# A spectral filter with gated convolution: the forward DFT by channel chunks, the rest by blocks of 512 positions, and part of the filter products on GpSimd

## The chip, the cores and the metric

The kernel runs on one core of a Trainium2 chip. The time is the device time of one execution in microseconds; three runs of the kernel before gave 344.11, 345.82 and 351.01 us, and their median is the time before. The engines are called PE (TensorE, matmuls; PEld are its weight loads), DVE (VectorE), ACT (ScalarE), POOL (GpSimd) and SP (SyncE, which here only issues DMAs).

## The reference

```python
# x (8, 3200, 256), filt_r and filt_i (1601, 256), float32
X = np.fft.rfft(x, axis=1)
y = np.fft.irfft(X * (filt_r + 1j * filt_i)[None], n=3200, axis=1)
# then, on y: a causal convolution of 5 taps per channel, as a gate
gate_pre[t] = sum(conv_w[k] * y_padded[t + k] for k in range(5))
gate = 1 / (1 + np.exp(-gate_pre))
out = (gate * (y @ w_val)) @ w_out        # (8, 3200, 256)
```

So each of eight batches is transformed over 3200 positions, multiplied by a filter, transformed back, convolved with a short filter whose sigmoid is a gate, multiplied by a value product, and multiplied by an output matrix.

## The kernel before

The DFT of 3200 points is split into 100 x 32: position n = 32a + r, with a from 0 to 99 and r from 0 to 31 (a phase). A batch goes through these stages, and each has a small function:

- `load_x`: eight loads per batch on the GpSimd queue, each of 4 phases (100 partitions x 4 x 256, cast from float32 to bf16). Tile `xt`, ten buffers.
- `s1`: the DFT over a, for 4 phases at once, two matmuls of 512 columns. Its moving operand is read in runs of 4 channels. `so` copies the result out of PSUM into one tile per batch.
- `turn`: four VectorE transposes of 32 x 32 blocks per batch (float32 words that hold two bf16 values), when all of `so` is there.
- `s2`: the DFT over r, for two of 13 frequency groups at a time (the last time one), so seven chunks `UCH` per batch. Four 64 x 64 matmuls stand side by side in the array. `xs` copies a chunk out of PSUM as bf16.
- `zed`: two products per chunk on VectorE, `za` with the real and `zb` with the imaginary part of the filter, from and to SBUF.
- `inva`: the inverse over one index, 16 matmuls per chunk, accumulated over `za` and `zb`. `ue` copies it out of PSUM, `wr` writes it to a scratch tensor `escr` in DRAM.
- `lv` reads `escr` back with another partition index, when all seven chunks are written; `ib` does the second inverse step for 4 phases at a time, and `ye` (ScalarE) copies y out of PSUM. y is held phase by phase as 36 x 100, the first four phases being a halo that `halo` copies on GpSimd.
- `conv`: 20 matmuls with diagonal matrices per chunk of 4 phases; a chunk needs only its own and the previous chunk of y. `gate` (ScalarE, sigmoid), `val` (matmuls of y with `w_val`), `gv` (VectorE, product of gate and value from PSUM), `outp` (8 matmuls of 256 columns), `oe` (copy out of PSUM) and `store` (two DMAs) follow, eight times per batch.

PSUM has four buffers of 128 x 1024 float32 that all stages take in turn. Copies out of PSUM go through the helper `copy` (L408 on ScalarE, L410 on VectorE), so many stages share one of these two lines.

The order of all instructions on all engines is written before the run: the class `Plan` holds a list of tasks with an assumed cost, the tasks that they depend on, the buffers that they take and give, and a rank. It runs through time with these costs and always takes the ready task of the lowest rank whose engine is free. The functions then emit their instructions in that order, and each engine works through its own in order. Where a copy can go to either engine, the plan chooses. Before the loop, `pool_setup` makes constants on GpSimd, loads batch 0 and the filters; `sp_setup` has SP double the filters in SBUF to the other partitions.

## Time and profile before

| what | value |
|---|---|
| median of three runs | 345.82 us (344.11 to 351.01) |
| the profiled execution's span | 344.8 us |
| PE busy | 288.3 us (84%) |
| ACT busy | 267.8 us (78%) |
| DVE busy | 256.4 us (74%) |
| POOL busy | 68.0 us (20%) |
| DMA, all queues | 70.91 MB, 206 GB/s on average |

The profiled execution's span lies 1.0 us below the median of the runs. The page gives busy times; a group of instructions has its line in the program, its engine, what it writes and reads, how many there are, the busy time and the mean time of one, and behind the bar the idle time of the engine just before them with what ended it. Busy times of neighbouring matmuls overlap, since a matmul's end is modelled, so what a stage costs on PE is better read from start to start in the timeline.

### The profile page before, as it was taken

The numbers are of one execution on the slowest core, as the hardware profiler recorded it, in microseconds if no ns is written. First come the engines' busy times: TensorE is split into PE (matmuls) and PEld (weight loads), VectorE is DVE, ScalarE is ACT, GpSimd is POOL, SyncE is SP. The second block draws the span as 40 slices with busy tenths as digits, with TensorE's granted clock in tenths as the row PEclk, the third lists the DMA queues.
The fourth block names the chain that finished last, engine by engine and source line by source line (L and its number), as shares of the span: only waits on it lengthen the run. The fifth ranks groups of instructions, "written<-read, shape, count | busy, mean of one in ns | idle before, by whom it ended". The sixth has DMA issues, their size and how long they took to land.

```text
span 344.8 us, 9785 instructions
## 1 busy us (share of the span) xinstructions
PE 288.3 (84%) x3988; PEld 191.6 (56%) x3988; DVE 256.4 (74%) x340; ACT 267.8 (78%) x309; POOL 68.0 (20%) x142
## 2 busy tenths in 40 slices
PE   2634677639999987999779997999999999999992
PEld 0023031326667755776457764776577677766762
DVE  4985477938698996889849994989798999734541
ACT  3954286928898987898849986998999789887663
POOL 8687455210112112110211011100100000001000
PEclk9999999969999999899989998999999999999997
DMA  6999999995899989898869969795677568778544
GB/s 95 155 168 163 213 192 195 206 238 168 199 232 247 272 233 231 245 229 251 170 200 207 271 176 250 214 245 171 199 208 221 156 204 261 234 214 248 160 144 143
DMA packets 57421, 70.91 MB, mean 206 GB/s; under 512 B 8608, under 2 KB 37152, under 8 KB 57376
## 3 DMA queue, kind: packets, MB, share of 16 engines
q1 hardware_dynamic: 45344, 55.20, 53.4%
q0 software_dynamic: 12032, 15.08, 29.0%
q8 instruction: 31, 0.51, 0.6%
q14 instruction: 14, 0.11, 0.1%
HBM read 43.78 MB, written 39.85 MB: 243 GB/s over the span
## 4 chain that ended last, share of the span: by engine, by line
PE 43%; DMA 24%; DVE 15%; ACT 7%; issue 4%; POOL 4%; SPq 1%; ACTq 0%; POOLq 0%; DVEq 0%
DMA vt<-escr 13%; PE ps L583 12%; PE ps L545 10%; DMA xt<-in_x_dram 6%; PE ps L563 6%; DVE tt L436 5%; DVE gv L573 5%; PE ps L417 5%; PE ps L518 5%; PE ps L477 4%; DMA fi_t<-in_filt_i_dram 3%; PE ps L446 3%; ACT o L408 2%; DVE xs L410 2%; POOL xt L161 2%
## 5 line engine op out<-in xcount | busy, mean ns | idle before, releaser
L573 DVE TENSOR_TENSOR gv<-ps,gt 128x800 bf16<-128x800 f32 x64 | 62.7, 980 | 19.9 <-PE ps L563 13.6
L408 ACT ACTIVATE o<-ps 100x1024 f32<-100x1024 f32 x59 | 61.0, 1035 | 16.9 <-PE ps L583 12.9
L410 DVE CAST xs<-ps 128x1024 bf16<-128x1024 f32 (+1 forms) x44 | 50.4, 1145 | 29.0 <-PE ps L446 29.0
L583 PE MATMUL ps<-wo_t,gv 128*100 128x256 bf16 x512 | 68.7, 278 | 2.7 <-DVE gv L573 1.1
L545 PE MATMUL ps<-yt,dg_t 64*64 64x400 bf16 x1280 | 67.3, 339 | 0.3
L408 ACT ACTIVATE so<-ps 128x1024 bf16<-128x1024 f32 x53 | 54.5, 1029 | 15.9 <-PE ps L417 11.1
L528 ACT ACTIVATE yt<-ps 128x800 bf16<-128x800 f32 x64 | 53.9, 846 | 15.9 <-PE ps L518 15.7
L583 PEld LDWEIGHTS <-gv 128*100 128x100 bf16 x512 | 54.5, 125 | 18.6 <-DVE gv L573 9.0
L161 POOL DMA_DIRECT2D xt<-in_x_dram x64 | 35.4, 556 | 124.5 <-PE ps L417 119.8
L554 ACT ACTIVATE gt<-ps 128x800 bf16<-128x800 f32 x64 | 54.1, 847 | 6.5 <-PE ps L545 5.3
L417 PE MATMUL ps<-xt,cf_t 100*128 100x512 bf16 x128 | 47.5, 462 | 12.2 <-DMA xt<-in_x_dram 11.2
L563 PE MATMUL ps<-yt,wv_t 128*128 128x400 bf16 x256 | 54.4, 335 | 0.5 <-ACT gt L554 0.5
L408 ACT ACTIVATE u<-ps 128x1024 bf16<-128x1024 f32 (+1 forms) x46 | 44.9, 982 | 7.2 <-PE ps L477 6.6
L518 PE MATMUL ps<-ci_t,vt 104*128 104x100 f16 x512 | 34.3, 212 | 16.5 <-DMA vt<-escr 16.4
L518 PEld LDWEIGHTS <-vt 104*128 104x128 bf16 x512 | 29.6, 100 | 30.1 <-DMA vt<-escr 19.8
L545 PEld LDWEIGHTS <-dg_t 64*64 64x64 bf16 x1280 | 34.5, 108 | 17.3 <-issue 4.2
L436 DVE STREAM_TRANSPOSE tt<-so 128x1024 f32<-128x1024 f32 x32 | 40.6, 1272 | 3.2 <-ACT so L408 3.2
L464 DVE TENSOR_TENSOR za<-xs,fr_t 128x1024 bf16<-128x1024 bf16 (+1 forms) x56 | 36.1, 649 | 1.4 <-ACT xs L408 0.2
L464 DVE TENSOR_TENSOR zb<-xs,fi_t 128x1024 bf16<-128x1024 bf16 (+1 forms) x56 | 35.5, 640 | 1.4 <-DMA fi_t<-in_filt_i_dram 1.4
L477 PE MATMUL ps<-zb,b_t 64*64 64x256 bf16 x416 | 29.7, 294 | 4.4 <-DVE zb L464 4.4
L477 PE MATMUL ps<-za,a_t 64*64 64x256 bf16 x416 | 30.3, 298 | 2.4 <-DVE za L464 2.1
L446 PE MATMUL ps<-tt,w_t 64*64 64x256 bf16 x416 | 24.2, 305 | 9.0 <-DVE tt L436 4.4
(93 smaller groups left out, 181.9 us busy)
## 6 DMA issues: line engine op xcount, KB each, us to landing
out_dram<-o SPq DMA_DIRECT2D x64, 384.0 KB
xt<-in_x_dram POOLq DMA_DIRECT2D x64, 200.0 KB, 6.7
escr<-u SPq DMA_DIRECT2D x48, 256.0 KB
vt<-escr SPq DMA_DIRECT2D x64, 192.0 KB
escr<-u SPq DMA_DIRECT2D x8, 128.0 KB
vt<-escr SPq DMA_DIRECT2D x64, 16.0 KB
out_dram<-o SPq DMA_DIRECT2D x64, 16.0 KB
fr_t<-in_filt_r_dram POOLq DMA_DIRECT2D x8, 56.0 KB, 4.7
```

Of the source, the lines that this page charges most:

```text
L408: nc.scalar.activation(dst, src, AF.Copy, **kw)
L410: nc.vector.tensor_copy(dst, src)
L417: nc.tensor.matmul(ps[:, 512 * h:512 * h + 512], lhsT=cf_t[0:L].rearrange("p h c i -> p (h c i)"), rhs=xv[:, DQ // 2 * h:DQ // 2 * h + DQ ...
L436: nc.vector.transpose(dst, src)
L464: (nc.vector if e == "DVE" else nc.gpsimd).tensor_tensor(z[:, :, 0:nm * D], xs_[:, :, 0:nm * D], f[:, :, m0:m0 + nm, :].rearrange("p h m d ...
L477: nc.tensor.matmul(ps[64 * h:64 * h + 64, 512 * t + D * a:512 * t + D * a + D], lhsT=tab[rows, h, m0 + a, :], rhs=zz[w][rows, h, D * a:D * ...
L518: nc.tensor.matmul(ps[:, o:o + L], lhsT=v[0:NV, a, 128 * dh:128 * dh + 128], rhs=ci_t[0:NV, :], start=True, stop=True)
L545: nc.tensor.matmul(ps[64 * dh:64 * dh + 64, 512 * r:512 * r + RC * L], lhsT=dg_t[rows, dh, k, :], rhs=y[rows, dh, RC * j + k:RC * j + k + ...
L554: nc.scalar.activation(g[...], ps[:, :].rearrange("p (h n) -> p h n", h=2)[:, :, 0:RC * L], AF.Sigmoid)
L563: nc.tensor.matmul(ps[:, 512 * eh:512 * eh + RC * L], lhsT=wv_t[:, dh, 128 * eh:128 * eh + 128], rhs=y[:, dh, H + RC * j:H + RC * j + RC, ...
L573: nc.vector.tensor_tensor(gv_[...], ps[:, :].rearrange("p (h n) -> p h n", h=2)[:, :, 0:RC * L], g[...], op=ALU.mult)
L583: nc.tensor.matmul(ps[0:L, D * a:D * a + D], lhsT=gv_[:, eh, L * a:L * a + L], rhs=wo_t[:, eh, :], start=(eh == 0), stop=(eh == 1))
```

## The change

- A load of x carries 8 phases, so there are four per batch, in six buffers. `s1` takes 32 channels and all 32 phases at a time: eight chunks per batch, each with four matmuls of 256 columns, one for each load. A transpose follows each chunk (eight per batch, of 512 words), with steps that put the result into one tile by frequency.
- The filters' real and imaginary parts stand in one tile, and one instruction forms both products of a chunk. In four of the seven chunks VectorE forms them straight from PSUM, so these chunks have no `xs` copy. In the other three (`ZG`), `xs` is still copied and GpSimd forms them; in batch 0 VectorE forms all seven.
- y is held in the order of the positions, in two tiles with four zeros ahead. `ib` works on 5 or 4 phases at a time (seven steps); the copy out of PSUM scatters its phases. The halo is gone; the scale 1/N has moved into tables.
- `conv`, `gate`, `val`, `gv`, `outp` and `store` work on blocks of 512 or 384 consecutive positions, seven per batch, and a block waits for the whole of y. `gv` writes its result so that `outp` has 128 positions at a step on the partitions: 50 matmuls of 256 columns per batch. A store is one DMA of 128 partitions.
- The plan keeps track of which of four PSUM buffers a task takes, has the DMA engines as an engine of its own, and takes ranks from a table.

```diff
+ZG = (1, 3, 5)
+ICH = [(0, 5), (5, 5), (10, 5), (15, 5), (20, 4), (24, 4), (28, 4)]
+BLK = [(0, 4), (4, 4), (8, 4), (12, 4), (16, 3), (19, 3), (22, 3)]
...
+PAR = dict(
+    PERIOD=20.7,
+    OFF=dict(cv=84.19, ia=48.09, ib=42.46, lv=-355.46, lx=-53.1, op=71.53, s1=-260.24, s2=45.97, vl=-551.16,
+             z=-229.99, zp=386.18),
+    STEP=dict(cv=1.785, ia=0.594, ib=5.658, lv=54.689, lx=0.786, op=8.159, s1=19.782, s2=1.912, vl=8.146,
+             z=1.876, zp=68.373),
+)
...
+    NXT, NSO, NXS, NZ, NU, NVB, NGB, NOB = 6, 3, 3, 3, 4, 4, 3, 4
...
+    f_t = cpool.tile([128, 2, 2, NM, D], BF16, name="f_t")
+    y_t = [cpool.tile([128, 2, H + N], BF16, name=f"y{n}") for n in range(2)]
...
+    def s1(b, q):
         ps = psum()
+        w = R // NX
+        for j in range(NX):
+            nc.tensor.matmul(ps[:, w * CQ * j:w * CQ * j + w * CQ],
                              lhsT=cf_t[0:L].rearrange("p h c i -> p (h c i)"),
+                             rhs=st["X", b, j][0:L, :, CQ * q:CQ * q + CQ],
+                             start=True, stop=True)
...
     def turn(b, q):
+        src = st.pop(("SO", b, q))[...].rearrange("p r w -> p (r w)").bitcast(FP32)
+        dst = st["T", b][...].rearrange("p i d -> p (i d)").bitcast(FP32)
+        V.transpose(dst.rearrange("p (i k) -> p k i", i=32)[:, CQ // 2 * q:CQ // 2 * q + CQ // 2],
+                    src.rearrange("p (r k) -> p k r", r=32))
...
+    def zed(b, u, e):
         m0, nm = UCH[u]
+        if e == "POOL":
+            eng, src = nc.gpsimd, st.pop(("XS", b, u))[:, :, 0:nm * D]
+        else:
+            eng, src = V, st.pop(("s2", b, u))[:, :].rearrange("p (h n) -> p h n", h=2)
+            src = src[:, :, 0:nm * D]
+        z = st["Z", b, u] = zpool.tile([128, 2, 2, 2 * D], BF16, name="z")
+        eng.tensor_tensor(z[:, :, :, 0:nm * D],
+                          src.unsqueeze(1).to_broadcast((128, 2, 2, nm * D)),
+                          f_t[:, :, :, m0:m0 + nm, :].rearrange("p w h m d -> p w h (m d)"),
+                          op=ALU.mult)
...
     def ye(b, i, e):
+        r0, nr = ICH[i]
         ps = st.pop(("ib", b, i))
+        copy(e, y_t[b % 2][:, :, H:H + N].rearrange("p h (n r) -> p h n r", r=R)
+             [:, :, :, r0:r0 + nr],
+             ps[:, :].rearrange("p (h n) -> p h n", h=2)[:, :, 0:nr * L]
+             .rearrange("p h (r n) -> p h n r", n=L))
...
     def conv(b, j):
+        m0, nm = BLK[j]
+                                 rhs=y[rows, dh, 128 * m0 + k:128 * m0 + k + 128 * nm],
...
+        V.tensor_tensor(
+            t[:, :, 0:nm, :].rearrange("p h a n -> p h n a"),
+            ps[:, :].rearrange("p (h n) -> p h n", h=2)[:, :, 0:128 * nm]
+            .rearrange("p h (n a) -> p h n a", a=nm),
+            gt[:, :, 0:128 * nm].rearrange("p h (n a) -> p h n a", a=nm), op=ALU.mult)
...
+        for a in range(nm):
             for eh in range(2):
+                nc.tensor.matmul(ps[:, D * a:D * a + D], lhsT=t[:, eh, a, :],
+                                 rhs=wo_t[:, eh, :], start=(eh == 0), stop=(eh == 1))
...
+        dst = out[b, 128 * m0:128 * m0 + 128 * nm, :].rearrange("(p a) d -> p (a d)", a=nm)
+        nc.sync.dma_start(out=dst, in_=o[:, 0:nm * D])
```

More of the change, by code (lines that the diff above doesn't have):

```diff
@@ L608, with act, dve, two @@
+    add = plan.add
+    def act(n):
+        return 0.2 + 0.00083 * n
+    def dve(n):
+        return 0.16 + 0.00105 * n
+    def two(n):
+        return {"ACT": act(n), "DVE": dve(n)}
+    def rank(s, b, k):
+        return s, b, k
     for b in range(B):
-        t0 = NCH * b
-        for j in range(NCH):
+        for j in range(NX):
             if b:
-                add(f"lx{b},{j}", {"POOL": 0.6}, t0 + j - 9, ["pool"], lambda e, b=b, j=j: load_x(b, j),
-                    take=("xt",), land=5.0)
-            dep = [f"lx{b},{j}"] if b else [f"x0{j}", "cfa"]
-            dep = dep + ([f"s1{b},{j - 1}"] if j else [])
-            add(f"s1{b},{j}", {"PE": 0.45}, t0 + j, dep, lambda e, b=b, j=j: s1(b, j),
-                take=("ps",) + (("so",) if j == 0 else ()), give=("xt",), mode=0)
-            add(f"so{b},{j}", two(0.97, 1.15), t0 + j, [f"s1{b},{j}"],
-                lambda e, b=b, j=j: so(b, j, e), give=("ps",))
@@ L677 @@
-    add("pool", {"none": 0.0}, -100, [], None, land=26.0)
-    add("wts", {"POOL": 8.0}, 8.5, ["pool"], lambda e: load_w())
-    for j in range(NCH):
-        add(f"x0{j}", {"none": 0.0}, -100, [], None, land=4.5 + 1.3 * j)
-    add("fl0", {"none": 0.0}, -100, [], None, land=26.0)
-    add("fl1", {"none": 0.0}, -100, [], None, land=34.0)
+                r = rank("lx", b, j)
+                add(f"li{b},{j}", {"POOL": 0.6}, r, ["pool"],
+                    lambda e, b=b, j=j: load_x(b, j), take=("xt",), land=1.0)
@@ new lines @@
+                add(f"lx{b},{j}", {"DMA": 2.2}, r, [f"li{b},{j}"], None, land=2.0)
+        for q in range(NQ):
+            r = rank("s1", b, q)
+            xs_ = [f"lx{b},{j}" for j in range(NX)] if b else [f"x0{NX - 1}", "cfa"]
+            add(f"s1{b},{q}", {"PE": 0.46}, r, xs_ + ([f"s1{b},{q - 1}"] if q else []),
+                lambda e, b=b, q=q: s1(b, q), take=("ps", "so"),
+                give=("xt",) * NX if q == NQ - 1 else (), mode=0)
+            add(f"so{b},{q}", two(1024), r, [f"s1{b},{q}"],
+                lambda e, b=b, q=q: so(b, q, e), give=("ps",), slot=f"s1{b},{q}")
+            add(f"t{b},{q}", {"DVE": 0.68}, r, [f"so{b},{q}"] + ([f"t{b},{q - 1}"] if q else []),
+                lambda e, b=b, q=q: turn(b, q), take=("t",) if q == 0 else (), give=("so",))
```

505 lines of the change are left out of this document (244 added, 261 removed).

## The prediction

> **What bounds the kernel now.** I read the busy rows of the page first, then the stretches, the lines, the waits, the chain and the timeline of the engines.
>
> ```profile
> span 344.8 us, 9785 instructions
> PE 288.3 (84%) x3988; PEld 191.6 (56%) x3988; DVE 256.4 (74%) x340; ACT 267.8 (78%) x309; POOL 68.0 (20%) x142
> ...
> 0.00:80.00 80.00, 45.21 (x459) 19.50 (x463) 53.93 (x111) 47.10 (x54) 43.54 (x91) 0.96 0.98 181
> 80.00:320.00 240.00, 224.74 (x3306) 159.65 (x3299) 194.10 (x222) 206.50 (x240) 24.42 (x51) 0.98 0.82 220
> 320.00:344.80 24.80, 18.35 (x234) 12.45 (x231) 8.41 (x9) 14.25 (x16) 0.00 (x0) 0.92 0.47 142
> ...
> 117.00:154.50 37.50, 34.76 (x513) 24.41 (x505) 31.07 (x37) 32.23 (x39) 5.75 (x12) 0.95 0.92 237
> 154.50:193.70 39.20, 34.06 (x499) 23.90 (x493) 30.47 (x35) 31.82 (x38) 5.54 (x11) 0.96 0.85 213
> 193.70:231.20 37.50, 34.07 (x499) 23.87 (x493) 30.44 (x35) 31.81 (x38) 4.58 (x10) 0.95 0.88 228
> 231.20:265.50 34.30, 32.70 (x496) 23.23 (x492) 30.45 (x35) 31.78 (x38) 1.10 (x3) 1.00 0.68 200
> ```
>
> The columns of a stretch are its length, then busy time of PE, its weight loads, DVE, ACT and POOL, the granted clock, the DMA share and GB/s. The last four stretches begin and end with a batch's first transpose, so each is one batch in the middle of the run, 37.1 us on average. In the one from 193.70 PE is busy for 34.07 of 37.5 us, ACT for 31.81, DVE for 30.44, and the DMA engines for 0.88 of the time (33 us). So PE sets the pace in the middle, with two engines and the DMA within 10% behind it. PE's idle time is 34.8 us in the first 80 us, 15.3 us in the next 240 and 6.4 us in the last 24.8: the start is where most is lost.
>
> ```profile
> PEld L518 <- DMA vt<-escr: 19.8, 8, 7.5
> PE ps L518 <- DMA vt<-escr: 16.4, 6, 7.3
> PE ps L417 <- DMA xt<-in_x_dram: 11.2, 8, 6.0
> ...
> 34.36 11.60 DMA xt<-in_x_dram
> ...
> 63.07 11.63 DMA vt<-escr
> ...
> 52.49 0.38 DVE L464 TENSOR_TENSOR zb<-xs,fi_t 128x512 bf16<-128x512 bf16 x1
> ...
> 79.12 1.89 PE L545 MATMUL ps<-yt,dg_t 64*64 64x400 bf16 x40
> ```
>
> These are waits (total, times, longest), then pieces of the chain and of the timeline. PE's largest waits are for the second batch's x and for the spectrum that comes back from DRAM. Batch 0's last filter product runs at 52.49, its spectrum is asked for only at 63.07, and its first convolution starts at 79.12.
>
> **The change, part by part.**
>
> 1. *Fewer output matmuls.* A block of 128 positions replaces 100 rows of a phase, so L583 goes from 64 matmuls of 256 columns per batch to 50.
>
> ```profile
> 163.18 1.03 PE L583 MATMUL ps<-wo_t,gv 128*100 128x256 bf16 x8
> 164.05 0.84 PE L563 MATMUL ps<-yt,wv_t 128*128 128x400 bf16 x4
> 164.73 0.61 PE L417 MATMUL ps<-xt,cf_t 100*128 100x512 bf16 x2
> 165.18 0.52 PE L518 MATMUL ps<-ci_t,vt 104*128 104x100 f16 x8
> ```
>
> From start to start eight of them take 0.87 us, 0.109 us each. 112 fewer give 112 x 0.109 = **-12.2 us** on PE, which is the pacing engine. The other matmuls keep their columns: convolution and value product stream 3200 columns per batch either way, in 7 blocks of 512 or 384 columns instead of 8 of 400; the forward DFT streams 8192. That its moving operand was read in runs of four elements costs nothing now: L417 takes 0.45 us for 1024 columns, as fast per column as L563 (0.68 for 1600). So longer runs bring nothing. The convolution will read at odd element offsets, which no row shows; I take 0. As a bound, two of five taps at half speed would be 0.4 x 6.9 us (8 groups of 0.86, the first two starts below) = 2.8 us a batch, 22 us in all.
>
> ```profile
> 153.63 1.04 PE L545 MATMUL ps<-yt,dg_t 64*64 64x400 bf16 x20
> 154.49 0.29 PE L446 MATMUL ps<-tt,w_t 64*64 64x256 bf16 x4
> 154.60 0.29 PE L477 MATMUL ps<-za,a_t 64*64 64x256 bf16 x4
> 154.71 0.29 PE L477 MATMUL ps<-zb,b_t 64*64 64x256 bf16 x4
> ```
>
> 2. *Vector and scalar work.*
>
> ```profile
> L573 DVE TENSOR_TENSOR gv<-ps,gt 128x800 bf16<-128x800 f32 x64 | 62.7, 980 | 19.9 <-PE ps L563 13.6 <-ACT gt L554 6.1
> L408 ACT ACTIVATE o<-ps 100x1024 f32<-100x1024 f32 x59 | 61.0, 1035 | 16.9 <-PE ps L583 12.9 <-ACT yt L528 1.5 <-DMA vt<-escr 1.4
> L410 DVE CAST xs<-ps 128x1024 bf16<-128x1024 f32 x38 | 46.4, 1222 | 28.8 <-PE ps L446 28.8
> L436 DVE STREAM_TRANSPOSE tt<-so 128x1024 f32<-128x1024 f32 x32 | 40.6, 1272 | 3.2 <-ACT so L408 3.2
> L464 DVE TENSOR_TENSOR za<-xs,fr_t 128x1024 bf16<-128x1024 bf16 x48 | 32.8, 689 | 1.2
> L464 DVE TENSOR_TENSOR zb<-xs,fi_t 128x1024 bf16<-128x1024 bf16 x48 | 32.5, 682 | 1.4 <-DMA fi_t<-in_filt_i_dram 1.4
> ```
>
> A product from PSUM costs what L573 costs per element. With a fixed part of 0.16 us, (0.98-0.16)/800 = 1.03 ns, so 2048 elements take 2.27 us and 1024 take 1.2. Now a chunk costs a cast (1.22 on DVE or about 1.03 on ACT) and two products (1.37), some 2.5 us together. The four VectorE chunks then cost 3 x 2.27 + 1.2 = 8.0 us a batch against 3 x 2.5 + 1.4 = 8.9: -0.9. The three GpSimd chunks keep the cast and drop 3 x 1.37 = -4.1 us. The output copies fall from 8192 to 6400 elements: 1.75 copies fewer, -1.8 us. Seven instead of eight copies of y, gates and products save little, since the elements stay. Transposes split in two gain four fixed parts, +0.5. In sum about -6.3 of the 62.2 us that DVE and ACT do in a middle batch (30.44 + 31.81). They are not the pace; their relief pays only as shorter waits, and I count it as **0** on the path. It also is the cover for price risks below: PE's batch becomes 34.07 - 1.5 = 32.5 us, so the two engines would need 2 x 32.5 - 56 = 9 us more per batch to overtake it.
>
> 3. *GpSimd products.* The nearest row is a one-input copy.
>
> ```profile
> L537 POOL COPY yt<-yt 128x396 bf16<-128x396 bf16 x16 | 7.9, 524 | 101.0 <-ACT yt L528 101.0
> L161 POOL DMA_DIRECT2D xt<-in_x_dram x64 | 35.4, 556 | 124.5 <-PE ps L417 119.8 <-DMA xt<-in_x_dram 2.1 <-DMA fi_t<-in_filt_i_dram 0.9
> ```
>
> At 1.3 ns an element 2048 elements take 2.7 us if both inputs stream together, 5.4 us if they take turns; I take 4.5, nearer the upper end because every element needs two reads. Three products and four load issues (0.56 each) make 16 us of POOL per batch, below the 33 that would make it a bound even at 5.4 (18.4). Queued behind a product on POOL are the next batch's loads of x, late by at most 5.4 us. The halo copies leave POOL. Cost on the path: **0**, because the spectrum of a batch is made while PE works on the batch before.
>
> [...]
>
> 4. *Access patterns.* The transpose's input step goes from 8 to 64 bytes, y is copied out of PSUM with a step of 400 bytes into runs of four or five values, and the gate product writes with a step of 256 bytes. No row shows such steps on DVE or ACT. The bounds: nothing, if they stream one element per cycle as now (L436 does with its step of 8), or twice the time per element. I take nothing, nearer to L436's row; the other end is the rival below.
>
> 5. *The start.* All four loads of batch 0 must land before the first DFT matmul, but the transposes then run chunk by chunk, so they end near 23 as now.
>
> ```profile
> 5.94 7.76 DMA xt<-in_x_dram
> ...
> 20.84 2.35 DVE L436 STREAM_TRANSPOSE tt<-so 128x1024 f32<-128x1024 f32 x2
> ...
> 28.28 1.29 DVE L464 TENSOR_TENSOR zb<-xs,fi_t 128x1024 bf16<-128x1024 bf16 x2 [1.40 <-DMA fi_t<-in_filt_i_dram]
> ...
> 34.22 28.63 SPq L498 DMA_DIRECT2D escr<-u  x8
> 63.07 0.34 SPq L508 DMA_DIRECT2D vt<-escr  x1
> ...
> 129.57 5.36 DMA vt<-escr
> ```
>
> The filters carry the same bytes, so the first product can start near 28. Seven products on VectorE alone take 6 x 2.27 + 1.2 = 14.8 us and end near 43, unless they are queued behind the second batch's work as now (52.49). Spectrum written by 48; read by 55, since the return takes 11.6 us in the start and 5.4 later; seven inverse groups of PE and y copied: first convolution near 60 instead of 79. But PE had done other work by then. Eight batches of 34.07 are 273 us, 243 of them lie after 80 (224.74 + 18.35), so 30 were done and 50 lost. In the new order it has done by 60 two batches' DFT and spectrum, 2 x (8 x 0.45 + 26 x 0.11) = 13, and batch 0's two inverse steps, 52 x 0.11 + 7 x 0.45 = 9, together 22, and 38 are lost: **-12 us**. Bounds: -18, if the return takes 5 us at once and the second batch's x is early, and +2, if the last product comes at 52.49 again (9.5 later) and the return takes 11.6 again (4.6 more).
>
> 6. *Convolution behind the whole inverse.* A block spans all phases, so its matmuls wait for all seven copies of y. PE would wait for the last of them, but the other y buffer's batch and the next batch's spectrum stand beside it: **0**; without that cover seven evacuations of some 0.8 us shared by two engines, 3 us a batch, 24 in all. SP issues 28 DMAs a batch instead of 39, off the path.
>
> Sum: 344.8 - 12.2 - 12 = 320.6 us of span, with the 15.3 and 6.4 us of idle later left as they are. The median of the runs shown, 345.82, lies 1.0 above that span, so about **322 us**. A change under 2% (7 us) is about what a measurement of this kernel cannot tell from none.
>
> **The rivals.**
>
> *Strided accesses are slow (slower).* Place: transposes, copies of y, gate products. If each element costs double: 4096 x 1.13 + 6400 x 0.83 + 6400 x 1.03 ns = 4.6 + 5.3 + 6.6 = 16.5 us a batch, so the two engines do 56 + 16.5 = 72.5, 36.3 each, 3.8 above PE's new 32.5, and with the same 3 us of idle a batch lasts 39.3 instead of 37.1 (the mean of the middle): 345.8 - 12 + 8 x 2.2 = 351 with even sharing. But the order is written before the run: DVE with its own 11.2 and half of the copies has 28 + 13.9 = 41.9 a batch, and without any idle that gives 334 + 8 x 4.8 = 372. I take **360**. It decides from 9 us a batch. For it: nothing here reads at such steps on those engines; against: PE's four-element runs are free. Chance 0.14.
>
> [...]
>
> *The DMA sets the pace.* Now 0.88 x 37.5 = 33 us of DMA per batch; bytes stay, only descriptors are longer. If landings grow late as the share nears 1, the batch stays at 37.1 and only the start gains: 346 - 12 = 334. For it: the waits for vt and x above. Against it: the rate has been 276 GB/s in a slice, above the 228 of that stretch. Chance 0.16.
>
> ```profile
> GB/s 95 155 168 163 213 192 195 206 238 168 199 232 247 272 233 231 245 229 251 170 200 207 271 176 250 214 245 171 199 208 221 156 204 261 234 214 248 160 144 143
> ```
>
> *The written order fits GpSimd badly.* If its products come 1 us later than PE's order assumes, three times in seven batches, PE waits 21 us: 343, no difference. The odd offsets of part 1 or the missing cover of part 6 would end there too. For it: POOL is nearly free of such work now; against: a whole batch of slack. Chance 0.10.
>
> *The relief pays.* If DVE and ACT, 6.3 us lighter, take away 10 of the 15.3 us of idle in the middle: 312. Chance 0.15.
>
> **How the numbers follow.** The forecast itself has 0.45, with its own range 316 to 336 from the start's bounds. Faster by over 2% (below 339): 0.41 of that, since costs counted as nothing can eat into it, the relief 0.15, the DMA 0.11 of its 0.16, making 0.67. Within 2%: 0.04 and 0.05 of these and 0.08 of the badly fitting order, 0.17. Slower: the strides 0.14 and 0.02 of the order, 0.16. The range goes from 304 (the relief and most of the start's -18) to 354 (the doubled strides, nearly evenly shared); what is beyond, some 0.15, is mostly the strides at their worst.
>
> **What would show it.** Right: 400 matmuls in the output group; PE busy near 276 us; products of 128x2048 on VectorE at 2.2 to 2.4 us; on POOL at 2.7 to 5.4; first convolution between 50 and 65 us; batch stretches of 33 to 36 us with PE over 90% busy. Wrong: transposes of 512 above 0.8 us, gate products of 1024 above 1.3 us or y copies of 1000 above 1.1; PE's largest wait in the middle naming GpSimd's z; or a DMA share above 0.95 in the middle.

## The result: slower by half, and the profile after

Four runs of the changed kernel gave 518.03 to 527.63 us, median 524.02, against 345.44 for four runs of the kernel before. The ratio is 1.505 (1.491 to 1.519). The executions fell into a faster and a slower state (518.03 and 521.75 against 526.3 and 527.63 us for the changed kernel), and all ratios here are formed from the faster one alone, while medians and some profiles (those of the changed kernel, `e7_spread_start`, `e11_no_gpsimd` and `e17_gate_tiles`) hold slower ones, so a median can lie a little beside its ratio. The forecast was 322.

First the page of the changed kernel: its busy row, the granted clock in 40 slices, the chain by engine and by line, and one group.

```profile
span 524.6 us, 9123 instructions
...
PE 334.8 (64%) x3785; PEld 205.2 (39%) x3812; DVE 452.7 (86%) x292; ACT 235.5 (45%) x246; POOL 126.7 (24%) x109
...
PEclk9999959879687967887878868888888787798886
...
DVE 48%; PE 27%; DMA 12%; issue 9%; POOL 2%; ACT 1%; DVEq 1%; SPq 0%; POOLq 0%; ACTq 0%
DVE gv L594 37%; PE ps L606 8%; PE ps L564 6%; PE ps L583 5%; DMA vt<-escr 4%; DVE tt L461 4%; DMA xt<-in_x_dram 3%; PE ps L445 3%; PE ps L545 3%; DMA wv_t<-in_moe_w_val_dram 2%; DVE z L492 2%; DVE o L192 1%; DVE y L192 1%; DVE u L192 1%; PE ps L505 1%
...
L492 POOL TENSOR_TENSOR z<-xs,f_t 128x2048 bf16<-128x2048 bf16 x21 | 85.3, 4065 | 215.7 <-ACT xs L190 169.3
```

VectorE has become the pace: 452.7 us busy where it had 256.4. One line, the gate product L594, stands on the chain for 37% of the span. TensorE computes less than before, but from 90 us on most slices show a granted clock of 0.7 or 0.8, and its busy time rises to 334.8. GpSimd's products take 4.07 us, inside the expected 2.7 to 5.4.

The groups of VectorE, with different shapes apart (busy time, mean ns of one, idle time before them), and the same view of ScalarE:

```profile
L594 DVE TENSOR_TENSOR gv<-ps,gt 128x1024 bf16<-128x1024 f32 x32 | 150.1, 4727 | 9.6 <-PE ps L583 6.3 <-issue 2.6 <-remote 0.6
L594 DVE TENSOR_TENSOR gv<-ps,gt 128x768 bf16<-128x768 f32 x24 | 85.7, 3587 | 12.4 <-PE ps L583 8.6 <-ACT so L190 2.3 <-ACT y L190 1.3
L461 DVE STREAM_TRANSPOSE tt<-so 128x512 f32<-128x512 f32 x64 | 69.2, 1110 | 9.1 <-ACT so L190 9.1
L492 DVE TENSOR_TENSOR z<-ps,f_t 128x2048 bf16<-128x2048 f32 x27 | 63.3, 2359 | 11.7 <-PE ps L472 6.8 <-DMA wv_t<-in_moe_w_val_dram 4.8
```
```profile
L190 ACT ACTIVATE y<-ps 128x1000 bf16<-128x1000 f32 x27 | 33.9, 1273 | 39.8 <-PE ps L545 39.8
```

Of the signs that the prediction had named as wrong, all three prices are there: transposes of 512 at 1.11 us (bound 0.8), gate products of 1024 at 4.73 (1.3), copies of y at 1.27 (1.1). Only one of them is large. The other two signs are not there: PE's largest wait names `gv` and not GpSimd's z, and the DMA share stays under 0.95 in the middle. Before, 64 gate products took 62.7 us; now 56 take 235.9. The first convolution, expected between 50 and 65 us, starts at 85.3.

The waits of PE (total, times, longest) and a stretch of one batch (columns as in the prediction):

```profile
PE ps L606 <- DVE gv L594: 71.8, 30, 3.9
```
```profile
180.00:240.00 60.00, 41.87 (x474) 25.78 (x477) 54.43 (x30) 28.34 (x30) 14.40 (x7) 0.77 0.52 155
```

A batch takes some 60 us instead of 37. VectorE works 54 of them, and the output matmuls wait for its product. The DMA share has fallen to 0.52, so nothing here points to the transfers.

### The profile page after: what moved, and what is told of

The parts are those of the page before. It is cut to its first block, busy times and chain, and to the rows that moved or that the text cites. A ratio compares the mean times of both kernels' runs of the same rounds, so it can differ in the third digit from the quotient of the medians.

```text
span 524.6 us, 9123 instructions
## 1 busy us (share of the span) xinstructions
PE 334.8 (64%) x3785; PEld 205.2 (39%) x3812; DVE 452.7 (86%) x292; ACT 235.5 (45%) x246; POOL 126.7 (24%) x109
## 4 chain that ended last, share of the span: by engine, by line
DVE 48%; PE 27%; DMA 12%; issue 9%; POOL 2%; ACT 1%; DVEq 1%; SPq 0%; POOLq 0%; ACTq 0%
DVE gv L594 37%; PE ps L606 8%; PE ps L564 6%; PE ps L583 5%; DMA vt<-escr 4%; DVE tt L461 4%; DMA xt<-in_x_dram 3%; PE ps L445 3%; PE ps L545 3%; DMA wv_t<-in_moe_w_val_dram 2%; DVE z L492 2%; DVE o L192 1%; DVE y L192 1%; DVE u L192 1%; PE ps L505 1%
## 5 line engine op out<-in xcount | busy, mean ns | idle before, releaser
L594 DVE TENSOR_TENSOR gv<-ps,gt 128x1024 bf16<-128x1024 f32 (+1 forms) x56 | 235.9, 4239 | 22.0 <-PE ps L583 15.0
L492 POOL TENSOR_TENSOR z<-xs,f_t 128x2048 bf16<-128x2048 bf16 x21 | 85.3, 4065 | 215.7 <-ACT xs L190 169.3
L606 PE MATMUL ps<-wo_t,gv 128*128 128x256 bf16 x400 | 70.7, 333 | 71.8 <-DVE gv L594 71.8
L564 PE MATMUL ps<-y,dg_t 64*64 64x512 bf16 (+1 forms) x1120 | 79.6, 418 | 16.5 <-DVE gv L594 16.1
L492 DVE TENSOR_TENSOR z<-ps,f_t 128x2048 bf16<-128x2048 f32 (+1 forms) x35 | 73.1, 2102 | 12.1 <-PE ps L472 7.2
L190 ACT ACTIVATE so<-ps 128x1024 bf16<-128x1024 f32 x53 | 53.4, 1024 | 61.1 <-PE ps L445 59.3
L574 ACT ACTIVATE gt<-ps 128x1024 bf16<-128x1024 f32 (+1 forms) x56 | 52.2, 933 | 60.3 <-PE ps L564 59.8
L461 DVE STREAM_TRANSPOSE tt<-so 128x512 f32<-128x512 f32 x64 | 69.2, 1110 | 9.1 <-ACT so L190 9.1
L445 PE MATMUL ps<-xt,cf_t 100*128 100x256 bf16 x256 | 53.0, 347 | 34.2 <-DMA xt<-in_x_dram 23.2
L190 ACT ACTIVATE y<-ps 128x1000 bf16<-128x1000 f32 (+1 forms) x45 | 49.0, 1099 | 57.3 <-PE ps L545 57.2
L583 PE MATMUL ps<-y,wv_t 128*128 128x512 bf16 (+1 forms) x197 | 64.2, 430 | 9.7 <-DVE gv L594 5.9
L545 PE MATMUL ps<-ci_t,vt 104*128 104x100 f16 x512 | 38.7, 233 | 24.4 <-DVE gv L594 19.4
L190 ACT ACTIVATE u<-ps 128x1024 bf16<-128x1024 f32 (+1 forms) x34 | 33.8, 997 | 33.9 <-PE ps L505 27.7
L583 PEld LDWEIGHTS <-wv_t 128*128 128x128 bf16 x224 | 24.5, 116 | 30.5 <-issue 21.7
```

The costliest lines, as they stand in the source:

```text
L190: nc.scalar.activation(dst, src, AF.Copy, **kw)
L445: nc.tensor.matmul(ps[:, w * CQ * j:w * CQ * j + w * CQ], lhsT=cf_t[0:L].rearrange("p h c i -> p (h c i)"), rhs=st["X", b, j][0:L, :, CQ * ...
L461: V.transpose(dst.rearrange("p (i k) -> p k i", i=32)[:, CQ // 2 * q:CQ // 2 * q + CQ // 2], src.rearrange("p (r k) -> p k r", r=32))
L492: eng.tensor_tensor(z[:, :, :, 0:nm * D], src.unsqueeze(1).to_broadcast((128, 2, 2, nm * D)), f_t[:, :, :, m0:m0 + nm, :].rearrange("p w h ...
L545: nc.tensor.matmul(ps[:, o:o + L], lhsT=v[0:NV, a, 128 * dh:128 * dh + 128], rhs=ci_t[0:NV, :], start=True, stop=True)
L564: nc.tensor.matmul(ps[64 * dh:64 * dh + 64, 512 * r:512 * r + 128 * nm], lhsT=dg_t[rows, dh, k, :], rhs=y[rows, dh, 128 * m0 + k:128 * m0 ...
```

## The experiments

### The gate product

My theory was the write: `gv` walks positions in the order n, a and writes one bf16 value at a time, 256 bytes from the last. The rivals were its reads (16 bytes apart in PSUM), and GpSimd working beside VectorE. (The expectations below call the first two theories W and R.)

**Write in order, let TensorE read at a step.** The product is written as it is read; the output matmuls take their weights from every fourth column.

```diff
-            t[:, :, 0:nm, :].rearrange("p h a n -> p h n a"), <value and gate in the same order>
+            t[:, :, 0:n], <value and gate as they lie>
-                nc.tensor.matmul(..., lhsT=t[:, eh, a, :],
+                nc.tensor.matmul(..., lhsT=t[:, eh, a:128 * nm:nm],
```

> The gate product is written in the order of the positions, one value behind the other, and the output matmuls pick every fourth (or third) column of it as their weights; nothing else is changed. Theory W (two-byte writes 256 bytes apart are slow on VectorE): the product of 1024 elements falls from 4.73 to about 1.2 us and that of 768 from 3.59 to 0.95, 8 x (4 x 3.5 + 3 x 2.6) = 174 us less of VectorE, and the kernel ends at 340 to 365 us, with the transposes still at 1.1 us. Theory R (the short inner runs of four elements and the order of reading are slow, whatever is written): here the order changes too, so the product gets fast as well; the next run tells them apart. [...] If weights picked with a step are slow to load, the output group's weight loads rise above 0.2 us each and the output group with them.

Measured: 360.12 us (355.17 to 362.35), ratio 1.037 (1.030 to 1.045). The busy row of that run, its gate product and its output group:

```profile
PE 277.2 (78%) x3785; PEld 184.3 (52%) x3812; DVE 282.6 (80%) x292; ACT 232.4 (66%) x246; POOL 126.6 (36%) x109
```
```profile
L595 DVE TENSOR_TENSOR gv<-ps,gt 128x1024 bf16<-128x1024 f32 x32 | 39.1, 1221 | 6.2 <-ACT y L190 3.0 <-ACT gt L574 1.8 <-PE ps L583 1.4
```
```profile
L605 PE MATMUL ps<-wo_t,gv 128*128 128x256 bf16 x400 | 54.1, 280 | 2.1 <-DVE gv L595 1.9
```

This change of layout gives back 164 of the 179 us. The product falls from 4.73 to 1.22 us. The 400 output matmuls take 280 ns each against 333, with a mean clock of 0.95 against 0.84. The next run, at 0.93, has its weights in order, and there they take 278: the stepped weights cost the matmuls nothing. The loads of these weights are longer than those of the value product's weights, which lie in order (112 ns against 99 in this run), but they stand beside other matmuls: 184.3 us of loads and 277.2 of matmuls fit in a span of 353.5. GpSimd is as busy as in the changed kernel (126.6 us against 126.7), so it doesn't make the product slow.

**Reads at a step, write in order.** The same as the changed kernel, but the walk is a, n for all three operands.

> The gate product is written one value behind the other in the tile that the output matmuls read as they do now, but its two inputs are read with steps of 16 bytes in PSUM and 8 bytes in SBUF, in runs of 128. Theory W: about 1.2 us for 1024 elements, the kernel within 10 us of the run with everything contiguous. If reads with steps are as dear as writes with steps: 3 us or more for 1024 elements, and the kernel above 450 us. [...]

Measured: 356.9 us (one run), the product of 1024 at 1218 ns:

```profile
L594 DVE TENSOR_TENSOR gv<-ps,gt 128x1024 bf16<-128x1024 f32 x32 | 39.0, 1218 | 6.9 <-ACT y L190 3.2 <-ACT gt L574 2.1 <-PE ps L583 1.6
```

Reads 16 bytes apart in PSUM and 8 bytes apart in SBUF cost nothing here (1218 ns against 1221); it is the write alone.

**Single instructions.** A kernel with nothing but these operations, four times each.

> Measures single instructions only; the reference's work is left out and the output is zeros. 1024 elements of the gate product: contiguous 1.2 us; written 256 bytes apart 4.7; read 16 and 8 bytes apart and written contiguous 1.2 by theory W, 2 or more if reads count as well. [...] Four-byte values (512): 0.7 up to a step of 8, 1.1 to 1.2 from 16 on. The copy of y on VectorE and ScalarE (1000 elements): 1.4 and 1.27 with both steps as in the kernel, 1.2 and 1.03 where only the reading is in steps of 400 bytes, if it is the writing that costs. Transposes of 512 words: 0.65 with steps of 8 bytes on both sides, 1.1 with the new steps; which side costs is open. GpSimd's product 4.1 us.

The product of 1024 values from PSUM, in order: written contiguously (L86), with the reads at a step (L88), and written with a step of 4 (L90), 8 (L91), 16 (L92) and 256 bytes (L87). Then three transposes of 512 words: with steps of 8 bytes on both sides, as before (L110), read at 64 and written at 8 (L111), and read at 64 and written at 512 bytes, as after (L113). The last two are ScalarE's copies of y, 1000 values: read 400 bytes apart and written in order (L105), and read in order and written 64 bytes apart (L107).

```profile
L86 DVE TENSOR_TENSOR bf<-ps,gt 128x1024 bf16<-128x1024 f32 x4 | 4.7, 1175 | 0.0
L88 DVE TENSOR_TENSOR gv<-ps,gt 128x1024 bf16<-128x1024 f32 x4 | 4.7, 1181 | 0.0
L90 DVE TENSOR_TENSOR bf<-ps,gt 128x1024 bf16<-128x1024 f32 x4 | 5.0, 1260 | 0.0
L91 DVE TENSOR_TENSOR bf<-ps,gt 128x1024 bf16<-128x1024 f32 x4 | 9.6, 2397 | 0.0
L92 DVE TENSOR_TENSOR bf<-ps,gt 128x1024 bf16<-128x1024 f32 x4 | 18.9, 4719 | 0.0
L87 DVE TENSOR_TENSOR gv<-ps,gt 128x1024 bf16<-128x1024 f32 x4 | 18.7, 4682 | 0.0
L110 DVE STREAM_TRANSPOSE tt<-so 128x512 f32<-128x512 f32 x4 | 2.9, 724 | 0.0
L111 DVE STREAM_TRANSPOSE tt<-so 128x512 f32<-128x512 f32 x4 | 4.2, 1045 | 0.0
L113 DVE STREAM_TRANSPOSE tt<-so 128x512 f32<-128x512 f32 x4 | 4.5, 1124 | 0.0
L105 ACT ACTIVATE yca<-pa 128x1000 bf16<-128x1000 f32 x4 | 4.0, 1004 | 0.0
L107 ACT ACTIVATE ya<-pa 128x1000 bf16<-128x1000 f32 x4 | 18.3, 4566 | 0.1
```

Against 1.18 us in order, a step of 4 bytes (four values on 16 bytes) took 1.26, of 8 bytes (two) 2.40 and of 16 bytes (one) 4.72; at 32 and at 256 bytes it was no more (4.63 and 4.68). A value alone cost 4.7 us / 1024 = 4.6 ns. At a step of 8 bytes I had expected either 1.2 or 4.7 us, and neither fits. The instructions stand right behind each other, and one behind a slow write showed as longer: the transpose of L110 took 0.91 us behind L87 and 0.66 to 0.67 the other three times. So rows that always stand there (512 four-byte values in order at 0.85 us, ScalarE's copy in order on both sides at 1.33) are not read as prices.

**The write alone, in the kernel before.** There are no GpSimd products in it, and nothing else of the change. The reads step as well, 400 bytes in PSUM and 200 in SBUF; alone, a VectorE copy of 1000 values that reads PSUM 400 bytes apart and writes in order took 1.16 us.

```diff
-            gv_[...], ps[...][:, :, 0:RC * L], g[...], op=ALU.mult)
+            gv_[...].rearrange("p h (a n) -> p h n a", n=L), <ps and g likewise>, op=ALU.mult)
```

> The kernel before with one thing of the change: the gate product (64 times, 128x800) walks its elements in the order of the rows, so that each value is written alone, 200 bytes from the last. By the price of 4.6 ns for each value written alone it takes 3.7 us instead of 0.98, VectorE is busy 256 + 64 x 2.7 = 429 us, and the kernel takes 460 to 510 us. Rival (the slow write needs the rest of the new kernel, its GpSimd products or its idle TensorE): the product stays under 2 us and the kernel under 400.

```profile
L573 DVE TENSOR_TENSOR gv<-ps,gt 128x800 bf16<-128x800 f32 x64 | 246.1, 3883 | 44.2 <-PE ps L563 35.3 <-ACT gt L554 7.5 <-issue 1.4
```

Measured: 550.53 us (two runs), ratio 1.600 (1.570 to 1.629). The product takes 3.88 us (3.7 expected) and VectorE is busy for 437.3 (429). So the write makes both versions of this kernel slow, and neither needs GpSimd's products for it. The time of the kernel was expected too low (460 to 510): VectorE is busy for only 80% of the span, and 44.2 of the other 108 us are its waits in front of this product.

**The transposes' layout back.** The changed kernel with the 8-byte steps of before for `so`, `turn` and `s2`, the gate product left slow.

> Only the first DFT's columns, the copy and the transposes are put back to the old layout: both sides of the transpose step by 8 bytes, the moving operand of the first DFT is read in runs of four, the copy writes runs of 32 values. [...] Rival (the transposes are slow because eight small ones have fixed costs): they stay near 1.1 us and the kernel near 520.

Measured: 518.74 us, ratio 1.491 (1.480 to 1.502). The transposes fell to 745 ns and VectorE's busy time by 19 us, but the kernel gained only some 5, with intervals that overlap: a miss, since 0.65 us a transpose and 490 to 505 for the kernel were expected. The transposes hold 4% of the chain above, some 20 us, and I had taken all of it as a gain. VectorE's idle time rose from 71.9 to 86.2 us instead, so most of what the transposes gave back became waits; what these waits were for is not shown. On the mended kernel the same edit gave 1.037 -> 1.020.

### What is left over the forecast

With both layouts mended (`e4_gv_turn`) the kernel should have been near the forecast, since every other price but that of the copies of y had come out near what was expected.

> The contiguous gate product of the first run together with the old transpose steps. The transposes are 0.35 us shorter, 64 of them 22 us of VectorE. Theory D (what is left over the forecast lies in returns from DRAM and in the start, not in VectorE): 346 to 358 us, waits of PE for vt and xt as before. Theory V (VectorE, 80% busy in the run with the contiguous product, still delays the second DFT): 330 to 345.

It took 353.59 us, ratio 1.020 (1.012 to 1.029), as theory D had it, and VectorE was down to 262.8 us busy, near the 256.4 of before. So 20 us less of VectorE's work brought 6.5, and some 30 remain over the forecast. The table gathers the runs that looked for them: the ratio to before, the start of the first convolution, and PE's waits for the returned spectrum (`vt`) and for x (`xt`), in us. The first wait of all, 6.6 to 7.1 us for batch 0's x, is put down by the profiles of `e6_start`, `e15_gate_more_x` and `e16_tiles_only` to a ScalarE instruction that the same matmul waits for; it is counted under x here, as in the other rows.

| run | ratio (95%) | first convolution | vt | xt |
|---|---|---|---|---|
| before | 1 | 79.1 | 16.4 | 11.2 |
| e4_gv_turn | 1.020 (1.012 to 1.029) | 82.3 | 27.7 | 24.4 |
| e6_start | 1.012 (1.003 to 1.021) | 82.5 | 30.2 | 13.7 |
| e8_x_cut | 0.919 (0.912 to 0.926) | 70.0 | 5.5 | 12.6 |
| e12_stores_cut | 0.977 (0.970 to 0.984) | 81.6 | 23.0 | 12.6 |
| e9_x_gated | 1.007 (1.002 to 1.013) | 67.2 | 6.6 | 17.0 |
| e14_gate_early | 1.010 (1.002 to 1.019) | 69.1 | 24.5 | 14.6 |
| e15_gate_more_x | **0.983 (0.975 to 0.991)** | 69.6 | 16.5 | 13.3 |
| e17_gate_tiles | 0.989 (0.984 to 0.994) | 69.0 | 7.4 | 17.3 |
| e16_tiles_only | 1.027 (1.019 to 1.034) | 89.5 | 29.0 | 17.7 |

**The start in the written order.** The plan is told that the second batch's x lands 9 us later, so that it doesn't put those matmuls ahead of batch 0's inverse.

```diff
-                    lambda e, b=b, j=j: load_x(b, j), take=("xt",), land=1.0)
+                    ..., take=("xt",), land=10.0 if b == 1 else 1.0)
```

> As e4_gv_turn; in the plan alone, the loads of x for the second batch are assumed to land 9 us later, so that PE's written order has batch 0's inverse before the second batch's first DFT. Theory P (the start's gain is lost because batch 0's last products stand behind matmuls that wait for x): the first convolution begins 6 to 15 us earlier and the kernel is 5 to 14 us under e4_gv_turn. Rival (the start is set by the filters and the return alone): within 4 us.

350.67 us ("the start version" from here on), 2.9 less, where theory P had 5 to 14. The wait for x fell from 24.4 to 13.7, but the first convolution stayed at 82.5. The reason stands in the timeline, here the rows of GpSimd's queue, of SP's and of PE:

```profile
27.80 1.10 POOL L221 DMA_DIRECT2D xt<-in_x_dram  x2
...
40.41 2.27 POOL L221 DMA_DIRECT2D xt<-in_x_dram  x4 [0.68 <-DMA wo_t<-in_moe_w_out_dram]
54.05 2.18 POOL L221 DMA_DIRECT2D xt<-in_x_dram  x4 [11.36 <-PE ps L445]
...
55.24 0.34 SPq L538 DMA_DIRECT2D vt<-escr  x1
...
64.00 0.99 PE L548 MATMUL ps<-ci_t,vt 104*128 104x100 f16 x10 [9.92 <-DMA vt<-escr]
```

Four loads of x (0.8 MB each, read) go out from 1 us ahead of the first request for the spectrum, since the last chunk of the batch before frees its x tiles at once; the spectrum takes 9 us. Counted through, with four loads per batch, these are the last two of the third batch and the first two of the fourth. The first two of the third went out at 40.41 with the second batch's last two, ahead of the spectrum's last writes: from 43 to 52 us (a slice of the page) the DMA engines are busy for 0.9 of the time or more here, against 0.7 to 0.8 in `e9_x_gated`, further down, which holds these loads back; in `e15_gate_more_x`, which does so too, the spectrum is asked for at 51.8 instead of 55.2. So loads of x stand ahead of the spectrum's writes and of its return. Before, in the middle of the run, the tiles came free one by one. Theory B of the following runs says that these bursts make the loss.

**Take x away.** The loads bring one phase of eight.

> The start version (350.7 us before) with seven eighths of x's loads left out from the third batch on: each load brings one phase of eight, and the first matmuls read that phase for all. Theory B (the burst of four 0.8 MB loads stands ahead of the spectrum's return and makes what is left over the forecast): PE's waits for the returned spectrum, 30.2 us there, fall under 12, and the kernel takes 322 to 334 us. Rival F (the returns are late for another reason, their own writes or the order): the waits stay over 22 and the kernel stays between 342 and 352.

316.54 us, 34 less than with x, and the waits for the spectrum nearly gone: theory B's way, and further than its range (322 to 334). The rows of the chain by line show it, of the version with x in full, then of the one without:

```profile
DMA vt<-escr 22%; PE ps L567 14%; PE ps L608 9%; PE ps L586 9%; PE ps L508 5%; PE ps L548 5%; PE ps L445 5%; DVE z L495 3%; PE ps L475 2%; DMA escr<-u 2%; ACT so L190 2%; ACT y L190 1%; ACT u L190 1%; SPq L538 1%; SPq L539 0%
```
```profile
PE ps L570 16%; PE ps L611 11%; PE ps L589 11%; DMA vt<-escr 10%; DMA xt<-in_x_dram 6%; PE ps L446 5%; PE ps L511 5%; PE ps L551 4%; DMA wv_t<-in_moe_w_val_dram 3%; ACT y L190 3%; PE ps L478 2%; DVE y L192 2%; DVE tt L468 2%; DMA f_t<-in_filt_r_dram 2%; POOL f_t L239 2%
```

The return of the spectrum holds 22% of 347.0 us, 76 us of the chain, and 10% of 312.9, 31 us, without x.

**Take the stores away instead.** This asks whether x counts as bytes or by its place.

> The start version (350.7 us) with seven eighths of each store of the result left out; x is loaded in full and at the same places. Theory T (all transfers together are the limit of the mended kernel; x is only a part of them): some 23 MB leave the queues, more than the x loads' 8.6, and the kernel takes 312 to 328 us, PE's waits for the returned spectrum fall under 12. Theory B (x's burst stands ahead of the return, the stores don't): the waits stay over 20 and the kernel between 338 and 350.

338.0 us. Rows of the DMA queues (packets, MB, share of 16 engines' span; q1 carries stores and spectrum, q0 mostly x), of the version in full, without x, and without stores:

```profile
q1 hardware_dynamic: 44704, 55.20, 48.0%
q0 software_dynamic: 7936, 15.08, 25.9%
```
```profile
q0 software_dynamic: 7936, 6.48, 14.6%
```
```profile
q1 hardware_dynamic: 44704, 32.26, 32.8%
```

The stores took 0.480 x 347.0 - 0.328 x 335.6 = 56 us of DMA time with them and brought 12; x took 0.259 x 347.0 - 0.146 x 312.9 = 44 us and brought 34. So the total of the transfers is not the limit, and theory T falls in this form; the cut stores ended at the low edge of what B allowed.

**Move x.** A copy of 32 values on GpSimd, from a late piece of the returned spectrum into the x tile, holds each load back until that piece has landed.

```diff
+        if b > 1:
+            nc.gpsimd.tensor_copy(xt[0:1, 0, 0:32], st["VK", b - 2, 3 + j][0:1, 0, 0:32])
         nc.gpsimd.dma_start(out=xt[0:L], in_=src)
```

> The start version with each x load held back, by a copy of 32 values on GpSimd out of the returned spectrum, until a late piece of the spectrum of two batches earlier has landed (pieces 3 to 6 for loads 0 to 3). Theory B: the waits for the spectrum fall from 30.2 to 8 to 18, the waits for x may grow by some us, the kernel takes 332 to 345 us, at or under the kernel before. Rival F: no gain, 348 to 358, the copies only add waits on GpSimd.

346.96 us, just above B's range. The wait for the spectrum fell to 6.6, further than B said, and the first convolution came 15 us earlier; but the kernel gained only some 2 to 4 us. Stretches from 80 to 280 us tell why: of the start version, of this one, and of the one without x.

```profile
80.00:280.00 200.00, 178.84 (x2591) 120.28 (x2586) 169.58 (x159) 154.22 (x165) 79.66 (x36) 0.95 0.74 215
```
```profile
80.00:280.00 200.00, 176.69 (x2423) 114.85 (x2416) 164.26 (x155) 141.95 (x151) 76.00 (x55) 0.94 0.79 215
```
```profile
80.00:280.00 200.00, 192.56 (x2881) 130.59 (x2881) 181.62 (x167) 163.89 (x176) 81.87 (x34) 1.00 0.69 218
```

PE idles for 21.2, 23.3 and 7.4 of these 200 us, and for 41.4, 35.4 and 34.5 of the 80 us ahead of them. Holding the loads back saves 6 us in the start and nothing in the middle: the time saved on the spectrum comes back as many small waits for x, for GpSimd's and VectorE's products and for copies. Of the 34 us that the version without x saves, 7 are idle time of the start, 14 of the middle and 2 of the end. The other 11 are PE's busy time (265.8 us for 276.9, the clock in this stretch being 1.00 for 0.95); 4 of them lie in the first DFT's matmuls, which read one phase eight times there. Two variants of the hold, two pieces earlier, and one piece earlier with eight x tiles instead of six:

> As the gated version (346.96 us), but each load waits for pieces 1 to 4 of the spectrum instead of 3 to 6. Theory T: the transfers only change places, 343 to 352 us, waits for the spectrum up by as much as those for x fall. Theory B: the waits for x (17.0 us, 13 of them at the start) lose the 4 of the later batches, and the kernel takes 335 to 343 us.

> The gated version with the loads waiting for pieces 2 to 5 and eight x tiles instead of six, so that all four loads of a batch can be out while the batch before still holds its four. Theory T: 343 to 352 us. Theory B: 333 to 343 us.

350.14 and 340.22 us: the first as theory T had it (the transfers only change places), the second as theory B. The second beats the kernel before by 1.7% (0.9 to 2.5%), less than the 2% that the prediction took as hard to tell from none. Whether its tiles or its hold did it:

> The start version (350.67 us) with eight x tiles instead of six and nothing held back. If the tiles alone made the 340.2 us of the last version, 336 to 344 us; if holding the loads back until the spectrum has landed is needed, 347 to 358, since x's burst is then free to go still earlier, and PE's waits for the spectrum stay over 20 us.

> Eight x tiles and loads that wait for pieces 3 to 6 of the spectrum (346.96 us with six tiles). If tiles and gate work together, 334 to 343 us and waits for the spectrum under 12; if the pieces 2 to 5 were what helped, 344 to 350.

Eight tiles with nothing held back give 356.48 us; all four of the third batch's loads go out at 46.1, where six tiles let out two at 40.4 and two at 54.1, ahead of most of the spectrum's writes, the spectrum is asked for at 63.8 instead of 55.2, and the first convolution slips to 89.5. With tiles and the first hold it is 344.56, just outside the range for tiles and hold together (334 to 343) and inside the one that gives the earlier pieces the credit (344 to 350). So the hold is needed and the tiles help only with it (1.007 -> 0.989 at the same hold); that an earlier piece adds to it (0.989 -> 0.983) is not shown, since the intervals overlap. None reaches the 316 without x; which property of x's loads costs the middle of the run stays open.

**Two misses on the way.** Each x load was given a place in the written order behind a GpSimd product of two batches earlier, with eight tiles, without and with the start's edit.

> As e4_gv_turn, and x has eight buffers instead of six, and the four loads of a batch are no longer issued together but one after each GpSimd product of two batches earlier. Theory B (the four loads that are issued together when the first DFT frees its buffers, 3.3 MB, stand in front of the spectrum's return): the waits of PE and its weight loads for vt (21.6 and 26.2 us in the first run) fall by more than half and the kernel ends 8 to 20 us under e4_gv_turn. If the returns are late for another reason (the chain of writes before them): within 4 us of e4_gv_turn.

> Both edits of e5_spread_x and e6_start on top of e4_gv_turn. If B and P hold and add up: 318 to 335 us, which is the forecast of the prediction at last; if they do not: 340 to 358.

355.62 and 382.46 us. By what was expected, the first came out against B, within 4 us of `e4_gv_turn`. But the order on the queue was no wait for anything else here: in the first, seven loads still went out together at 37.1, and PE still waited 20.3 us for the spectrum and 25.9 for x; in the second one load stood on GpSimd for 57.8 us with the products behind it, and the time lies above both of its ranges. Neither put theory B to the test; the held-back version was made for that.

**Old and new, without x.** Whether the kernel before was bound by TensorE, as the prediction read it:

> The kernel before with three quarters of x's loads left out from the third batch on (each load of four phases brings one). If TensorE bounded the kernel before, as the prediction read it, only its waits for the returned spectrum (9.0 us between 80 and 280) can go: 332 to 344 us. If the transfers bounded it, it gains as the start version did without x: 312 to 328 us.

335.49 us, ratio 0.967 (0.958 to 0.976): the gain of a kernel that mostly waits for TensorE. It is a third of what the new design gained, with three quarters of the loads left out there against seven eighths here.

**No products on GpSimd** (`ZG = ()` on the start version).

> The start version with all seven products on VectorE from PSUM and none on GpSimd. 21 products of 2.28 us come to VectorE, 48 us, and 21 copies of about 1.05 us leave ScalarE; both together have 494 us now and would have some 520, 260 each. Theory (relief of VectorE and ScalarE is not on the path once the write is mended): 345 to 358 us, within 2% of the start version. Rival (GpSimd's three products carry the new kernel): 362 to 385 us, with VectorE over 300 us busy.

364.94 to 373.31 us, without an interval, and 14 us or more above the start version. GpSimd's three products do carry time, as the rival said, though VectorE's busy time rose only to 283.7, under the rival's 300. Of the 23 us that the profile's span is longer, PE is busy for 14, at a mean clock of 0.92 against 0.94, and idle for 9; its waits for the spectrum (32.7) and for x (12.7) are about those of the start version. So the price of the relief is not cleanly measured.

## Why the prediction was wrong, point by point

Between the forecast (322) and the median (524.02) lie 202 us. The gate product's layout brought back 164 of them and the transposes' layout 6.5 more (point 4); the 31.6 that remain lie mostly in the start (point 5).

1. *Output matmuls*: right. 400 in the group, and PE busy for 277.2 us (near 276 expected) with the clock back at a mean of 0.95; the odd offsets of the convolution cost nothing that shows there.
2. *Products from PSUM*: right, 2.36 us against 2.27. The relief was smaller than 6.3 us a batch: VectorE and ScalarE fell from 524.2 to 494.5 us in the version with both layouts mended, 3.7 a batch. Counting it as nothing was doubtful, as the version without GpSimd shows.
3. *GpSimd*: right, 4.07 us between 2.7 and 5.4, 4.5 taken.
4. *Access patterns*: **the step that failed**, in two ways. I took nothing, because the transposes' 8-byte steps (L436: 1272 ns for 1024 words, 1.24 ns a word; the prediction's "one element per cycle" is in no view) and TensorE's four-element runs (0.45 us for 1024 columns) counted as free; the first are steps of 4-byte words, two to 16 bytes, the second are reads by another engine. Neither was near a lone 2-byte write. And the other bound, twice the time, had no row behind it: the product took 3.9 times, (4.73 - 1.22) x 4 + (3.59 - 0.95) x 3 = 22 us a batch, where the rival had 6.6. The rival had the place right and the price a third, so even it ended at 360. The transposes were inside the bound (1.11 against 0.72 at the old steps, 1.5 times), and the copies of y paid for their short runs, not for reading 400 bytes apart: on ScalarE 1.00 us for contiguous writes read so, 1.22 for runs of five read so, and 1.24 for runs of five read in order.
   The single instructions show how much the size of the element matters: 512 4-byte words took 0.66 us at a step of 8 bytes and 1.03 at 16, while 1024 2-byte values took 2.40 at 8 bytes, twice their 1.18 in order. Reads at a step in PSUM cost nothing there: 1.18 us with and without.
5. *The start*: **the second step that failed**. The sum took 12 us less idle time of PE in the first 80 us, 22.8 instead of 34.8; the start version has 41.4. That is 18.6 of the 26.4 us by which its span (347.0) exceeds the 320.6 of the sum; 7.0 are idle time later and 0.8 PE's busy time. The first convolution came at 82 us instead of 60, even with the written order mended. The condition named (products behind the second batch's work) did hold in the first mended version; the greater part was the bursts of x ahead of the spectrum's writes and return, which the prediction had not seen although it listed that tiles and loads change. Held back, the convolution comes at 67 to 70, but only 6 us of the idle time go with it; what holds the rest of the start is not shown.
6. *Convolution behind the whole inverse, at 0*: right in its own terms. In the start version no convolution waits for a copy of y, and the 3 us a batch of the bound are nowhere. What had no term is the wait ahead of the inverse: PE waits for the spectrum for 15.6 us between 80 and 280, against 9.0 before; holding x back lowers that to 6.6, and other waits take its place.

The rival *the DMA sets the pace* (334) does not hold for the mended kernel either: the sum of the transfers does not set its time, since 56 us less of stores brought 12 and 44 us less of x brought 34. Of the rival *the written order fits GpSimd badly* nothing shows: in the changed kernel and in the start version PE has no wait for GpSimd's z.

## What to carry to other kernels

A price bound needs a row of the same kind: the same engine, the same side (read or write) and the same size of element; where none exists, the bound of a scattered 2-byte write is four times, as measured here on VectorE (4.72 us against 1.18) and ScalarE (4.57 against 1.00), not twice. Let the engine that writes do so in order, and let TensorE do the stepping when it loads its weights (here 112 ns a load against 99, and 280 ns a matmul against 278). When a tiling frees several tiles at once, look at what their reloads will stand in front of.

## What the runs showed of the hardware

- 2-byte values written alone on their 16 bytes took 4.6 ns each on VectorE (4.72 us for 1024 values 16 bytes apart, against 1.18 contiguous) and the same on ScalarE (4.57 us for 1000 values 64 bytes apart, against 1.00 contiguous).
- Reads at a step were free in products and copies: PSUM at 16 bytes (1.18 us) and 400 bytes (1.16 on VectorE, 1.00 on ScalarE), gates in SBUF at 8. Weights read at 8 bytes (at 6 in the blocks of 384) loaded in 112 ns, against 99 for the value product's weights in order, and the matmuls with them took no longer (280 ns against 278). In the transposes reads at a step did cost: 512 words read at 64 bytes and written at 8 took 1.05 us, against 0.72 with 8 bytes on both sides.
- TensorE's granted clock was lower in the kernel in which it waited more: 0.77 to 0.86 in the stretches of 60 us from 60 to 480 us after (PE busy for 39 to 42 of each), 0.95 in the start version between 80 and 280 us (178.8 of 200) and 1.00 there without x (192.6); matmuls that take 277 us in the first mended version took 335. Waiting is not all of it: in the first 80 us, with PE busy for 38.6 and 38.5 of them, the clock was 0.87 in `e6_start` and 0.68 in `e12_stores_cut`.
- DMA time was not worth the same everywhere: 44 us less of x's loads brought 34 us, 56 us less of stores 12. In the start, with loads of x going out 1 us ahead of the request, PE began on the first piece of the spectrum 8.8 us after it, at 64.0 us; with these loads held back it began at 55.2 us.
